# Pooled attention and a cosine-gated MLP on one core: the attention of each batch put between the second matmuls of the preceding token tile, the first matmul in pairs of columns over three two-bank PSUM tiles

## The chip, the cores and the metric

The kernel runs on one core of a Trainium2 chip. The metric is the device time of one execution in microseconds (us); the time shown for a kernel is the median of its runs.

## The reference, cut to what matters

Eight batches of 576 tokens (4608 tokens in all), 8 heads of 64. Keys and values are averaged over groups of 8 tokens, so that each head has 72 pooled keys; the attention's output, 4608 x 512, goes through an MLP without bias whose gate is h * cos(h).

```python
k_p = k.reshape(B, H, Sp, pool, D).mean(axis=3)      # Sp = 72, pool = 8
v_p = v.reshape(B, H, Sp, pool, D).mean(axis=3)
scores = scale * np.matmul(q, k_p.transpose(0, 1, 3, 2))
attn = np.exp(scores - np.max(scores, axis=-1, keepdims=True))
attn = attn / (np.sum(attn, axis=-1, keepdims=True) + 1e-09)
x = np.matmul(attn, v_p)          # then tokens x (heads * 64) = 4608 x 512
h = x @ w_in                      # w_in 512 x 2048
return (h * np.cos(h)) @ w_out    # w_out 2048 x 512
```

## The kernel before, in words

The program has two stages, one after the other, and Tile's scheduler sets the order of the instructions inside each engine's queue.

**Attention (lines 73 to 146).** For each batch, q, k and v come in chunks of 128 tokens (lines 82, 93, 99), each of them as rows of 256 bytes; ScalarE casts each chunk to bf16 (lines 84, 95, 101). TensorE transposes q (line 87), VectorE copies the transposed chunk out of PSUM with a stride of four elements on the side that it writes (line 90). TensorE pools k and v by a product with a 0/1 matrix (`pool_ext`, lines 96 and 102), and transposes the pooled keys (line 113). Then, for each pair of heads `pj` and each segment of 512 or 64 tokens, the scores of one head at a time go into `sT_ps` (line 132), ScalarE takes the exponential (line 135), two products give the sum of the exponentials, spread over 64 partitions (`cs_ps`, line 138), and the weighted values (`ao_ps`, line 140). VectorE takes the reciprocal of the sum (line 143) and multiplies (line 145); the result lies transposed in `xT_tiles`, 128 channels by 4608 tokens, four of them.

**MLP (lines 150 to 205).** The weights are loaded and cast (lines 155, 156, 162, 163). For each of nine tiles of 512 tokens, 16 chunks of 128 hidden channels are worked through: four matmuls of 512 columns into `h_ps` (line 178), the cosine as a sine with a bias (line 186), the product with h (line 189), and four matmuls into the four output blocks `out_ps` (line 193), which gather over all 16 chunks. At the tile's end ScalarE copies the four blocks out (line 204) and they are stored (line 205). There are thus 64 "first" matmuls (line 178) and 64 "second" ones (line 193) for each tile, 1152 in all.

PSUM has eight banks of 128 partitions x 512 f32. In the MLP stage three are used for `h_ps` and four for `out_ps`; the attention's PSUM pool is closed first (line 148).

Of the kernel before, what the change touches and what calls it, by code (L numbers as in the profile page):

```python
# [10 lines left out]
BF16 = mybir.dt.bfloat16  # L12


@with_exitstack
def kernel(
# [11 lines left out]
    POOL = 8  # L28
# [5 lines left out]

    assert d_model == moe_w_in.shape[0]
    assert moe_w_out.shape == (d_ff, d_model)
    assert out.shape == (n_tokens, d_model)
# [9 lines left out]
    ones_mat = consts.tile([128, 128], BF16, name="ones_mat")  # L47
    nc.gpsimd.memset(ones_mat, float(POOL))

# [3 lines left out]
    n_pool_cols = 136  # L53
    pool_ext = consts.tile([128, n_pool_cols], BF16, name="pool_ext")
    nc.gpsimd.memset(pool_ext, 1.0)
    nc.gpsimd.affine_select(pool_ext, pool_ext, pattern=[[-8, n_pool_cols]],
                            compare_op=mybir.AluOpType.is_ge, fill=0.0,
                            base=512, channel_multiplier=1)
    nc.gpsimd.affine_select(pool_ext, pool_ext, pattern=[[8, n_pool_cols]],
                            compare_op=mybir.AluOpType.is_gt, fill=0.0,  # L60
                            base=-504, channel_multiplier=-1)

    xT_pool = ctx.enter_context(tc.tile_pool(name="xT", bufs=1))
    xT_tiles = [xT_pool.tile([128, n_tokens], BF16, name=f"xT_{ki}") for ki in range(KCH)]

    s_chunk_bounds = list(range(0, S, 128)) + [S]
    NSC = len(s_chunk_bounds) - 1

    asb = ctx.enter_context(tc.tile_pool(name="asb", bufs=2))
    attn_ctx = ExitStack()  # L70
    aps = attn_ctx.enter_context(tc.tile_pool(name="aps", bufs=1, space=bass.MemoryType.PSUM))

    for b in range(B):
        qT = asb.tile([128, S, KCH], BF16, tag="qT")
        kp_ps = aps.tile([Sp, H * D], FP32, name="kp_ps", tag="kp_ps")
        vp_ps = aps.tile([Sp, H * D], FP32, name="vp_ps", tag="vp_ps")
        for ci in range(NSC):
            s0, s1 = s_chunk_bounds[ci], s_chunk_bounds[ci + 1]
            sc = s1 - s0
            pool_slice = pool_ext[:sc, 64 - 16 * ci: 64 - 16 * ci + Sp]  # L80
            qc_f = asb.tile([128, H, D], FP32, tag="qc_f")
            nc.sync.dma_start(out=qc_f[:sc, :, :], in_=q[b, :, s0:s1, :].rearrange("h s d -> s h d"))
            q_chunk = asb.tile([128, H * D], BF16, tag="q_chunk")
            nc.scalar.copy(out=q_chunk[:sc, :], in_=qc_f[:sc, :, :].rearrange("s h d -> s (h d)"))  # L84
            qT_ps = aps.tile([128, KCH, 128], BF16, name="qT_ps", tag="qT_ps")
            for pj in range(KCH):
                nc.tensor.matmul(qT_ps[:128, pj, :sc],  # L87
                                 q_chunk[:sc, pj * 128:(pj + 1) * 128], identity[:sc, :sc],
                                 is_transpose=True)
            nc.vector.tensor_copy(out=qT[:, s0:s1, :].rearrange("p s j -> p j s"),  # L90
                                  in_=qT_ps[:128, :KCH, :sc])
# [12 lines left out]

        kp = asb.tile([Sp, H * D], BF16, tag="kp")
        nc.scalar.copy(out=kp, in_=kp_ps[:Sp, :])
        vp = asb.tile([Sp, H * D], BF16, tag="vp")
        nc.scalar.copy(out=vp, in_=vp_ps[:Sp, :])

        kpT = asb.tile([128, KCH, Sp], BF16, tag="kpT")  # L110
# [125 lines left out]
```

## Time and profile before

| what | us |
|---|---|
| median of 3 runs (lowest, highest) | 547.68 (547.28, 548.22) |
| span of the profiled execution | 544.7 |
| attention and weights, to the first matmul of line 178 | 273.0 |
| MLP, from there to the span's end | 271.7 |
| busy: TensorE, VectorE, ScalarE, GpSimd | 442.7, 296.6, 247.2, 1.6 |

The span of the profiled execution runs from its first to its last instruction; its own device time is not among the three runs, and the median of these lies 3.0 us above its span. PE stands for TensorE's matmuls, PEld for its weight loads, DVE for VectorE, ACT for ScalarE, POOL for GpSimd, SPq for the queue of the engine that issues the loads and stores. In a group's row, "x" is the count, then come busy time and the mean time of one; behind the bar, the idle time of the engine just before, and what ended it. The mean time of a matmul is its latency: matmuls overlap, so that eight of them which take 0.38 us each can stand in 1.73 us.

### The profile page before, as it was taken

Reading aid. Unit: us, or ns where it says so; the run is one execution under the profiler, and the core shown is the slowest. Engines: PE = TensorE matmul, PEld = TensorE weight load, DVE = VectorE, ACT = ScalarE, POOL = GpSimd, SP = SyncE. Lnnn points to the kernel's source line nnn. Section 1 sums busy time; section 2 is a strip of 40 time slices with the busy share of each in tenths; the row PEclk is TensorE's granted clock in tenths of the full one; section 3 lists DMA queues with packets and bytes.
Section 4 is the critical chain, followed back from the end, with each engine's and each line's share of the span. In section 5 each row is a group of like instructions: output and inputs, shape, how many; then the busy total and the mean of one; then the engine's idle time right before and its main releaser. Section 6 shows DMA issues by size and latency. Waiting matters only on the chain.

```text
span 544.7 us, 5181 instructions
## 1 busy us (share of the span) xinstructions
PE 442.7 (81%) x1808; PEld 167.6 (31%) x1808; DVE 296.6 (54%) x332; ACT 247.2 (45%) x454; POOL 1.6 (0%) x11
## 2 busy tenths in 40 slices
PE   3675866758686676745599999999999999999994
PEld 1222223222222222212233333333333433343331
DVE  2387676867867686786865334433443344334431
ACT  4554454555445464522233535453444435443543
POOL 1000000000000000000000000000000000000000
PEclk9999999999999999999999999999999999999998
DMA  9955538464465755705043201010020202020202
GB/s 191 207 113 124 119 87 154 102 136 91 97 135 124 125 119 118 238 1 193 0 137 95 78 1 73 5 51 27 1 77 1 77 1 77 1 77 2 77 1 77
DMA packets 120601, 46.47 MB, mean 85 GB/s; under 512 B 113408, under 2 KB 113408, under 8 KB 120064
## 3 DMA queue, kind: packets, MB, share of 16 engines
q1 hardware_dynamic: 120576, 46.15, 35.4%
q8 instruction: 14, 0.23, 0.2%
q14 instruction: 11, 0.09, 0.0%
HBM read 36.70 MB, written 9.44 MB: 85 GB/s over the span
## 4 chain that ended last, share of the span: by engine, by line
PE 71%; ACT 9%; issue 7%; DVE 7%; DMA 4%; SPq 1%; ACTq 0%
PE out_ps L193 24%; PE h_ps L178 22%; PE sT_ps L132 9%; ACT expT L135 8%; PE cs_ps L138 6%; DVE qT L90 5%; PE ao_ps L140 3%; PE qT_ps L87 2%; PE kp_ps L96 2%; DMA kc_f<-in_k_dram 2%; PE vp_ps L102 1%; DMA wo_f<-in_moe_w_out_dram 1%; DMA vc_f<-in_v_dram 1%; DVE inv L143 1%; DVE w_in L156 1%
## 5 line engine op out<-in xcount | busy, mean ns | idle before, releaser
L189 DVE TENSOR_TENSOR g_sb<-h_ps,cos_sb 128x512 bf16<-128x512 f32 x144 | 99.5, 691 | 153.1 <-ACT cos_sb L186 153.1
L186 ACT ACTIVATE cos_sb<-h_ps,half_pi 128x512 f32<-128x512 f32 x144 | 99.1, 689 | 143.9 <-PE h_ps L178 143.9
L178 PE MATMUL h_ps<-xT,w_in 128*128 128x512 bf16 x576 | 142.8, 384 | 2.7 <-DVE xT L145 2.7
L193 PE MATMUL out_ps<-w_out,g_sb 128*128 128x512 bf16 x576 | 142.0, 380 | 2.5 <-DVE g_sb L189 2.3
L143 DVE RECIPROCAL inv<-cs_ps 128x512 f32<-128x512 f32 x64 | 120.4, 1922 | 33.9 <-PE cs_ps L138 33.9
L135 ACT ACTIVATE expT<-sT_ps 72x64 bf16<-72x64 f32 (+1 forms) x128 | 52.0, 407 | 90.3 <-PE sT_ps L132 65.9
L178 PEld LDWEIGHTS <-w_in 128*128 128x128 bf16 x576 | 56.9, 99 | 72.7 <-issue 6.2
L132 PE MATMUL sT_ps<-qT,kpT 64*72 64x64 bf16 (+1 forms) x128 | 56.1, 438 | 25.1 <-ACT expT L135 22.1
L193 PEld LDWEIGHTS <-g_sb 128*128 128x128 bf16 x576 | 46.2, 97 | 92.7 <-DVE g_sb L189 54.8
L90 DVE COPY qT<-qT_ps 128x512 bf16<-128x512 bf16 (+1 forms) x40 | 47.1, 1178 | 46.3 <-PE qT_ps L87 46.3
L138 PE MATMUL cs_ps<-expT,ones_mat 72*64 72x64 bf16 (+1 forms) x128 | 41.0, 427 | 18.5 <-ACT expT L135 17.6
L87 PE MATMUL qT_ps<-identity,q_chunk 128*128 128x128 bf16 (+1 forms) x160 | 22.9, 289 | 31.1 <-DVE qT L90 24.2
L140 PE MATMUL ao_ps<-expT,vp 72*64 72x64 bf16 (+1 forms) x128 | 40.7, 437 | 0.0
L84 ACT CAST q_chunk<-qc_f 128x512 bf16<-128x512 f32 (+1 forms) x40 | 24.5, 612 | 20.5 <-PE qT_ps L87 16.6
L87 PEld LDWEIGHTS <-q_chunk 128*128 128x128 bf16 (+1 forms) x160 | 14.1, 125 | 56.7 <-issue 39.9
L96 PE MATMUL kp_ps<-k_chunk,pool_ext 128*72 128x512 bf16 (+1 forms) x40 | 24.8, 620 | 5.5 <-ACT k_chunk L95 5.4
L102 PE MATMUL vp_ps<-v_chunk,pool_ext 128*72 128x512 bf16 (+1 forms) x40 | 24.7, 616 | 4.8 <-ACT v_chunk L101 4.5
L132 PEld LDWEIGHTS <-kpT 64*72 64x72 bf16 x128 | 14.8, 132 | 39.0 <-issue 30.0
L138 PEld LDWEIGHTS <-ones_mat 72*64 72x64 bf16 x128 | 13.9, 132 | 41.4 <-issue 39.8
L95 ACT CAST k_chunk<-kc_f 128x512 bf16<-128x512 f32 (+1 forms) x40 | 24.5, 611 | 2.5 <-DMA kc_f<-in_k_dram 2.5
L101 ACT CAST v_chunk<-vc_f 128x512 bf16<-128x512 f32 (+1 forms) x40 | 24.4, 610 | 2.5 <-DMA vc_f<-in_v_dram 2.5
L145 DVE TENSOR_TENSOR xT<-ao_ps,inv 128x512 bf16<-128x512 f32 x64 | 24.2, 419 | 0.0
(24 smaller groups left out, 79.7 us busy)
## 6 DMA issues: line engine op xcount, KB each, us to landing
out_dram<-out_sb SPq DMA_DIRECT2D x36, 256.0 KB, 2.2
qc_f<-in_q_dram SPq DMA_DIRECT2D x32, 256.0 KB, 3.2
kc_f<-in_k_dram SPq DMA_DIRECT2D x32, 256.0 KB, 3.8
vc_f<-in_v_dram SPq DMA_DIRECT2D x32, 256.0 KB, 3.8
wi_f<-in_moe_w_in_dram SPq DMA_DIRECT2D x4, 1024.0 KB, 5.5
wo_f<-in_moe_w_out_dram SPq DMA_DIRECT2D x16, 256.0 KB, 2.7
qc_f<-in_q_dram SPq DMA_DIRECT2D x8, 128.0 KB, 2.8
kc_f<-in_k_dram SPq DMA_DIRECT2D x8, 128.0 KB, 3.0
```

What stands on the lines that cost most here:

```text
L87: nc.tensor.matmul(qT_ps[:128, pj, :sc], q_chunk[:sc, pj * 128:(pj + 1) * 128], identity[:sc, :sc], is_transpose=True)
L90: nc.vector.tensor_copy(out=qT[:, s0:s1, :].rearrange("p s j -> p j s"), in_=qT_ps[:128, :KCH, :sc])
L96: nc.tensor.matmul(kp_ps[:Sp, :], lhsT=pool_slice, rhs=k_chunk[:sc, :], start=(ci == 0), stop=(ci == NSC - 1))
L132: nc.tensor.matmul(sT_ps[:Sp, :sl], lhsT=kpT[ph0:ph1, pj, :Sp], rhs=qT[ph0:ph1, seg0:seg1, pj])
L135: nc.scalar.activation(out=expT[:Sp, :sl], in_=sT_ps[:Sp, :sl], func=mybir.ActivationFunctionType.Exp, scale=scale / POOL)
L138: nc.tensor.matmul(cs_ps[ph0:ph1, :sl], lhsT=ones_mat[:Sp, :D], rhs=expT[:Sp, :sl])
L140: nc.tensor.matmul(ao_ps[ph0:ph1, :sl], lhsT=vp[:Sp, h * D:(h + 1) * D], rhs=expT[:Sp, :sl])
L143: nc.vector.reciprocal(out=inv[:, :sl], in_=cs_ps[:, :sl])
L178: nc.tensor.matmul(h_ps[:128, :m_len], lhsT=w_in_sb[ki][:, fc * 128:(fc + 1) * 128], rhs=xT_tiles[ki][:, mi:mi + m_len], start=(ki == 0), ...
L186: nc.scalar.activation(out=cos_sb[:128, :m_len], in_=h_ps[:128, :m_len], func=mybir.ActivationFunctionType.Sin, bias=half_pi[:128, :1])
L189: nc.vector.tensor_mul(out=g_sb[:128, :m_len], in0=h_ps[:128, :m_len], in1=cos_sb[:128, :m_len])
L193: nc.tensor.matmul(out_ps[ms][:m1 - m0, :d_model], lhsT=g_sb[:128, m0:m1], rhs=w_out_sb[fc][:, :d_model], start=(fc == 0), stop=(fc == FFC ...
```

## The change

The function is written anew; only the constants, the launch and the mathematics stay. What it does:

- **Order by hand.** `tc.manual_schedule()` makes each engine's queue the order in which the code is written. Waits for data and for free buffers are still put in.
- **Loads.** k and v come as one tile of 72 partitions, each with 8 heads x 8 tokens x 64 (runs of 2 KB, line 77); 512 of a batch's 576 tokens of q come as four neighbouring tokens to a partition (runs of 1 KB, line 84), the other 64 apart (line 87). Token 4n+t of a batch stands in column n of group t, and the stores at line 240 undo this by a stride in DRAM.
- **Pooling by three adds** (lines 111 to 113: 2048, 1024 and 512 elements for each of 72 partitions) instead of a matmul; the casts of q (lines 119, 121) and these adds run on GpSimd, except that batch 0 is pooled on VectorE. GpSimd also casts the four parts of `w_out` (line 264).
- **Attention in eight steps** of two heads by 288 tokens. `scores` (line 166) puts the two heads into the two banks of one PSUM tile and takes one exponential over both, 72 x 576. `values` (line 177) makes the two sums and the two weighted values in the two banks of `banks[2]`; the reciprocal becomes a logarithm and an exponential of its negative on ScalarE (lines 187, 189), and VectorE multiplies (line 191). `k_transpose`, `q_transpose` and `q_transpose_rem` come first, and copy by VectorE. In line 143 both sides of the copy are walked in the order in which they stand, so that the block of token group t and head pair j in PSUM goes to head pair t and token group j in `qT`.
- **MLP.** For a tile, `up` runs eight times: eight matmuls into a two-bank tile (three of these, `banks`, used in turn), one sine of 128 x 1024, one product of 128 x 1024 into `g_sb`, which holds the whole tile's 16 chunks and has one buffer. Then 64 second matmuls, 16 for each of four output blocks, with two single banks in turn (`obanks`), copied out by VectorE (line 231).
- **Interleaving.** Between the second matmuls of tile t, the attention of batch t+1 is issued: its three transposes before matmuls 4, 8 and 12, and then its sixteen pieces (`scores` and `values`) from matmul 16 to 53, every two or three. Batch 0 stands alone ahead of tile 0; tiles 7 and 8 have nothing between. The activation tables are switched twice a tile (lines 206, 209).

On TensorE, inside a batch of the attention stage before (around its row 312 in that engine's queue: `sT_ps` are scores, `cs_ps` sums, `ao_ps` weighted values, `kp_ps` and `vp_ps` pooled keys and values):

```order
L132 LDWEIGHTS kpT
L132 MATMUL sT_ps<-qT,kpT 72x64
L138 LDWEIGHTS ones_mat
L138 MATMUL cs_ps<-expT,ones_mat 64x512
L138 LDWEIGHTS ones_mat
L138 MATMUL cs_ps<-expT,ones_mat 64x512
L102 LDWEIGHTS pool_ext
```

and now, in tile 0, batch 1 (`obank` takes second matmuls, `bank` 94 and 95 the scores, 96 sums and weighted values):

```order
L226 MATMUL obank_98<-w_out_sb,g_sb 128x512
L171 LDWEIGHTS kpT
L171 MATMUL bank_94<-qT,kpT 72x288
L171 LDWEIGHTS kpT
L171 MATMUL bank_94<-qT,kpT 72x288
L226 LDWEIGHTS g_sb
L226 MATMUL obank_98<-w_out_sb,g_sb 128x512
```

The matmuls of the attention, which stood among others of the attention, now stand in groups of two or four between second matmuls; each group changes the shape of the weights (64x72 or 72x64 against 128x128) and changes it back.

On GpSimd, the last rows of the whole program before were

```order
L51 MEMSET half_pi 128x1
L55 MEMSET pool_ext 128x136
L56 AFFINE_SELECT pool_ext<-pool_ext 128x136
L59 AFFINE_SELECT pool_ext<-pool_ext 128x136
```

and now, from the cast of batch 0's q through batch 1:

```order
L119 CAST q_bf<-q_main 128x8x4x64
L121 CAST q_rem_bf<-q_rem 64x512
L264 CAST w_out_sb<-w_st 128x2048 x4
L111 TENSOR_TENSOR kv_st<-kv_st 72x8x256
L112 TENSOR_TENSOR kv_st<-kv_st 72x8x128
L113 TENSOR_TENSOR kp<-kv_st 72x512
L119 CAST q_bf<-q_main 128x8x4x64
L121 CAST q_rem_bf<-q_rem 64x512
L111 TENSOR_TENSOR kv_st<-kv_st 72x8x256
L112 TENSOR_TENSOR kv_st<-kv_st 72x8x128
L113 TENSOR_TENSOR vp<-kv_st 72x512
```

GpSimd, which only set up constants, now has four weight casts and then eight instructions for each batch in one queue, those of batch 1 behind the weight casts.

The diff, cut to its core (the new file's lines; what only declares is left out):

```diff
+    def pool_kv(b, which, eng, halves=1):
...
+            eng.tensor_tensor(out=s[:, :, 0:4, :], in0=s[:, :, 0:4, :], in1=s[:, :, 4:8, :], op=ADD)
+            eng.tensor_tensor(out=s[:, :, 0:2, :], in0=s[:, :, 0:2, :], in1=s[:, :, 2:4, :], op=ADD)
+            eng.tensor_tensor(out=dst[:, i * hs:(i + 1) * hs, :], in0=s[:, :, 0, :], in1=s[:, :, 1, :], op=ADD)
...
+    def q_transpose(b, bank):
...
+        ps = bank.rearrange("p a n -> p (a n)").bitcast(BF16).rearrange("p (t j n) -> p t j n", t=4, j=KCH)
+        for t in range(4):
             for pj in range(KCH):
+                nc.tensor.matmul(ps[:, t, pj, :], qb[:, t, 2 * pj:2 * pj + 2, :].rearrange("p h d -> p (h d)"),
+                                 identity, is_transpose=True)
+        c0 = col_of(b, 0)
+        nc.vector.tensor_copy(out=qT[:, :, c0:c0 + 512].rearrange("p j (t n) -> p j t n", t=4),
+                              in_=ps.rearrange("p t j n -> p j t n"))
...
+    def scores(b, i):
+        pj, sg = i // 2, i % 2
+        kpT, qT = att["kpT", b], att["qT", b]
+        pair = banks[(i + 1) % 2]
+        for hp in range(2):
+            nc.tensor.matmul(pair[:Sp, hp, :SEG], lhsT=kpT[hp * 64:hp * 64 + 64, pj, :],
+                             rhs=qT[hp * 64:hp * 64 + 64, pj, sg * SEG:(sg + 1) * SEG])
+        ex = asb.tile([Sp, 2, SEG], BF16, name="ex", tag="ex")
+        nc.scalar.activation(out=ex, in_=pair[:Sp, :, :SEG], func=ACTF.Exp, scale=scale / POOL)
...
+    def values(b, i):
...
+        cs, ao = banks[2][:, 0, :SEG], banks[2][:, 1, :SEG]
+        for hp in range(2):
+            nc.tensor.matmul(cs[hp * 64:hp * 64 + 64, :], lhsT=ones[:Sp, :], rhs=ex[:, hp, :])
+        for hp in range(2):
+            nc.tensor.matmul(ao[hp * 64:hp * 64 + 64, :], lhsT=vp[:, 2 * pj + hp, :], rhs=ex[:, hp, :])
+        lnc = asb.tile([128, SEG], FP32, name="lnc", tag="lnc")
+        nc.scalar.activation(out=lnc, in_=cs, func=ACTF.Ln)
+        inv = asb.tile([128, SEG], FP32, name="inv", tag="inv")
+        nc.scalar.activation(out=inv, in_=lnc, func=ACTF.Exp, scale=-1.0)
+        c0 = b * S + sg * SEG
+        nc.vector.tensor_mul(out=xT[:, pj, c0:c0 + SEG], in0=ao, in1=inv)
...
+    def up(t, fp):
+        h = banks[fp % 3]
+        for j in range(2):
+            fc = 2 * fp + j
             for ki in range(KCH):
+                nc.tensor.matmul(h[:, j, :], lhsT=w_in_sb[:, ki, fc * 128:(fc + 1) * 128],
+                                 rhs=xT[:, ki, t * TILE:(t + 1) * TILE],
+                                 start=(ki == 0), stop=(ki == KCH - 1))
+        cos = msb.tile([128, 2, TILE], FP32, name="cos", tag="cos")
+        nc.scalar.activation(out=cos, in_=h, func=ACTF.Sin, bias=half_pi[:, :1])
+        nc.vector.tensor_mul(out=g_sb[:, 2 * fp:2 * fp + 2, :], in0=h, in1=cos)
...
+    for cg in range(4):
+        st = w_stage[cg]
+        nc.vector.tensor_copy(out=w_in_sb[:, :, cg * 512:(cg + 1) * 512], in_=st)
+        if cg + 2 < 4:
+            w_stage.append(load_w_in(cg + 2))
+    for cg in range(4):
+        st = load_w_out(cg)
+        nc.gpsimd.tensor_copy(out=w_out_sb[:, cg * 4:(cg + 1) * 4, :], in_=st)
+    load_kv(1, "k", k)
+    load_q(1)
+    load_kv(1, "v", v)
+    pool_kv(1, "k", nc.gpsimd)
+    cast_q(1, nc.gpsimd)
+    pool_kv(1, "v", nc.gpsimd)
+    for t in range(NT):
+        b = t + 1
+        for fp in range(FFCH // 2):
+            up(t, fp)
...
+            fill = [(4 + 4 * i, f) for i, f in enumerate(early)]
+            fill += [(16 + (i * 5) // 2, f) for i, f in enumerate(main)]
...
+        for n, (ms, fc) in enumerate(mms):
+            while fi < len(fill) and fill[fi][0] <= n:
+                fill[fi][1]()
+                fi += 1
+            down_mm(ms, fc)
+            if fc == FFCH - 1:
+                down_out(t, ms)
```

The two weight staging buffers (`wst`) are shared by `w_in` and `w_out`, four parts of 1 MB each: a part's load waits until the part two places earlier has been cast. VectorE's casts of `w_in` stand behind batch 0's last product (line 191) in its queue.

More of the change, by code (lines that the diff above doesn't have):

```diff
@@ L12 @@
 BF16 = mybir.dt.bfloat16
+ACTF = mybir.ActivationFunctionType
+ADD = mybir.AluOpType.add
+POOL = 8
+TILE = 512
 @with_exitstack
@@ L27 @@
     B, H, S, D = q.shape
-    POOL = 8
     Sp = S // POOL
@@ L45 @@
     make_identity(nc, identity)
-    ones_mat = consts.tile([128, 128], BF16, name="ones_mat")
-    nc.gpsimd.memset(ones_mat, float(POOL))
+    ones = consts.tile([128, D], BF16, name="ones")
+    nc.gpsimd.memset(ones, float(POOL))
     half_pi = consts.tile([128, 1], FP32, name="half_pi")
     nc.gpsimd.memset(half_pi, math.pi / 2.0)
[L53 to L69, printed above, removed]
```

268 lines of the change are left out of this document (149 added, 119 removed).

## The prediction

> **What bounds the kernel now.** I read the page first, then the table by stage, the groups of instructions by shape, and the timeline at four places. Page and table by stage (span, then PE, PEld, DVE, ACT and POOL busy, clock, DMA share, GB/s):
>
> ```profile
> span 544.7 us, 5181 instructions
> PE 442.7 (81%) x1808; PEld 167.6 (31%) x1808; DVE 296.6 (54%) x332; ACT 247.2 (45%) x454; POOL 1.6 (0%) x11
> PEclk9999999999999999999999999999999999999998
> 3.00:239.00 236.00, 163.88 (x594) 58.37 (x595) 163.26 (x146) 121.03 (x255) 0.00 (x0) 1.00 0.64 131
> 273.00:539.00 266.00, 263.55 (x1152) 102.91 (x1151) 105.51 (x159) 116.16 (x179) 0.00 (x0) 1.00 0.12 44
> ```
>
> Two stages, each about half of the span. In the first no engine is full: PE and DVE are busy 69% of the time, ACT 51%, and they wait for each other. In the second PE is full, 1152 matmuls in 266 us, 0.231 us each. What a matmul costs in each stage stands in the groups by shape, in the chain that ended last, and in the timeline where the second stage begins:
>
> ```profile
> L178 PE MATMUL h_ps<-xT,w_in 128*128 128x512 bf16 x576 | 142.8, 384 | 2.7 <-DVE xT L145 2.7
> L138 PE MATMUL cs_ps<-expT,ones_mat 72*64 72x512 bf16 x64 | 26.3, 625 | 3.5 <-ACT expT L135 2.6
> L87 PE MATMUL qT_ps<-identity,q_chunk 128*128 128x128 bf16 x128 | 19.9, 304 | 22.8 <-DVE qT L90 16.1 <-ACT q_chunk L84 6.5
> 476.41 1.90 PE out_ps L193 x8
> 478.31 1.73 PE h_ps L178 x8
> 272.97 4.98 PE L178 MATMUL h_ps<-xT,w_in 128*128 128x512 bf16 x12 [2.65 <-DVE xT L145]
> 257.25 0.64 PE L138 MATMUL cs_ps<-expT,ones_mat 72*64 72x512 bf16 x2
> 257.68 0.64 PE L140 MATMUL ao_ps<-expT,vp 72*64 72x512 bf16 x2
> ```
>
> A run of eight first matmuls takes 1.73 us, 0.216 each; a run of eight second ones 1.90. In the attention the same 512 columns take 625 ns where the MLP shows 384, and the first twelve of the MLP take 4.98 us, 0.41 each: PE runs at about half speed there, and for the first dozen dense matmuls after it, though the granted clock reads 1.00 throughout. And two sums for the two halves of PSUM's partitions lie on top of each other: two pairs, four matmuls, from 257.25 to 258.32, the second pair 0.43 after the first.
>
> So the floor of the change is PE at full speed: 1152 x 0.216 = 249 us, plus the attention's matmuls.
>
> **The first matmuls.** `up` has 64 in a row: 64 x 0.216 = 13.8 us. Beside them run eight sines and eight products of 1024:
>
> ```profile
> L186 ACT ACTIVATE cos_sb<-h_ps,half_pi 128x512 f32<-128x512 f32 x144 | 99.1, 689 | 143.9 <-PE h_ps L178 143.9
> L189 DVE TENSOR_TENSOR g_sb<-h_ps,cos_sb 128x512 bf16<-128x512 f32 x144 | 99.5, 691 | 153.1 <-ACT cos_sb L186 153.1
> L135 ACT ACTIVATE expT<-sT_ps 72x512 bf16<-72x512 f32 x64 | 38.0, 593 | 43.8 <-PE sT_ps L132 43.8
> L135 ACT ACTIVATE expT<-sT_ps 72x64 bf16<-72x64 f32 x64 | 14.1, 220 | 46.5 <-PE ao_ps L140 22.9 <-PE sT_ps L132 22.1
> L145 DVE TENSOR_TENSOR xT<-ao_ps,inv 128x512 bf16<-128x512 f32 x32 | 20.1, 627 | 0.0
> L145 DVE TENSOR_TENSOR xT<-ao_ps,inv 128x64 bf16<-128x64 f32 x32 | 6.7, 210 | 0.0
> 536.18 0.38 PE L178 MATMUL h_ps<-xT,w_in 128*128 128x512 bf16 x1
> 536.60 0.69 ACT L186 ACTIVATE cos_sb<-h_ps,half_pi 128x512 f32<-128x512 f32 x1 [2.07 <-PE h_ps L178]
> 537.32 0.69 DVE L189 TENSOR_TENSOR g_sb<-h_ps,cos_sb 128x512 bf16<-128x512 f32 x1 [2.07 <-ACT cos_sb L186]
> 538.06 1.04 PE L193 MATMUL out_ps<-w_out,g_sb 128*128 128x512 bf16 x4 [1.50 <-DVE g_sb L189]
> ```
>
> By the two shapes ACT takes 0.83 ns a column over a start of 0.17 us, DVE 0.93 over 0.15. The sine of 1024 then costs 0.69 + 0.43 = 1.12, the product 0.69 + 0.48 = 1.17. A two-bank tile comes free 0.2 + 1.12 + 1.17 + 0.1 = 2.6 us after its matmuls end; PE wants it 2 x 1.73 = 3.45 us after. Hidden, 0.9 to spare; without that, PE would pay the difference eight times a tile. The last product ends 2.6 us after `up`, and matmul 14 wants it 3.0 after: hidden too.
>
> **The second matmuls with the attention.** 64 x 0.216 = 13.8 again. A pair of 288 columns costs 288/512 x 0.216 = 0.121 if its halves overlap, as the sums do above (for the halves of the rows, in `scores`, no row shows it: at most 0.243, and I take 0.121). Eight steps of one such pair and of two in `values`: 8 x 0.363 = 2.9.
>
> Each of the sixteen pieces changes the shape of the weights and back. At the slow speed the timeline shows one such change, from scores to sums:
>
> ```profile
> 250.45 0.64 PE L132 MATMUL sT_ps<-qT,kpT 64*72 64x512 bf16 x1
> 251.02 0.13 PEld L138 LDWEIGHTS <-ones_mat 72*64 72x64 bf16 x1 [0.44 <-issue]
> L193 PEld LDWEIGHTS <-g_sb 128*128 128x128 bf16 x576 | 46.2, 97 | 92.7 <-DVE g_sb L189 54.8 <-issue 1.6
> ```
>
> The load begins 0.57 after a matmul of 0.43 of columns, and takes 0.13: up to 0.27 for a change. At full speed the nearest row is the run of 1.90 against 1.73: weight loads of `g_sb` there wait on a semaphore, are not pulled ahead, and such a run costs 0.17 more, though nothing changes its shape. Between nothing and 0.27 I take 0.16, the full speed's row: 32 x 0.16 = 5.1 us a tile. [...]
>
> A step is five second matmuls, three pairs and four changes: 1.08 + 0.36 + 0.64 = 2.08 us. Beside it goes a ring through one PSUM tile, `banks[2]`: sums, logarithm 0.17 + 288 x 0.83 ns = 0.41, exponential 0.41, product 0.15 + 0.27 = 0.42, next sums. With 0.4 from PE's start to ACT (536.18 to 536.60 above) and 0.14 for three handovers, 1.78 us: hidden, by 0.3. ACT itself needs 0.65 + 0.41 + 0.41 = 1.47 a step. The reciprocals that go are DVE's busiest group, and their place is taken by 0.82 of ACT a step, under PE.
>
> Ahead of the steps stand 16 second matmuls (3.45), 24 transposes (2.0: q's sixteen took 19.9/128 = 0.155 each at the slow speed, 0.10 is my estimate for the full one, and 0.05 for the eight smaller) and two changes: 5.8 of PE. But the copy of `qT` is later: q's last transpose ends 8 x 0.216 + 0.2 + 1.6 + 0.4 = 3.9 us into the stretch.
>
> ```profile
> L90 DVE COPY qT<-qT_ps 128x512 bf16<-128x512 bf16 x32 | 41.3, 1291 | 41.7 <-PE qT_ps L87 41.7
> L143 DVE RECIPROCAL inv<-cs_ps 128x512 f32<-128x512 f32 x64 | 120.4, 1922 | 33.9 <-PE cs_ps L138 33.9
> L186 ACT ACT_TABLE_LOAD x1 | 1.3, 1283 | 5.0 <-PE h_ps L178 5.0
> ```
>
> The copy of 2048 per partition costs 2048 x 0.93 + 0.15 = 2.06 if written in runs, up to 4.7 at the strided row's (1291 - 150)/512 = 2.2 ns. I take 2.06, since runs are what the product's row has. With the copy of the rest (0.39) the first scores start at 6.5. The table loads, 1.28 twice a tile, lie where ACT has 5 us free (sines end at 1.4, the first exponential is at 6.8) and under the last 11 second matmuls (2.4 us); exposed, 14 would cost 18.
>
> The rest: 48 x 0.216 + 2.9 + 5.1 = 18.4. **A tile with attention:** 13.8 + 6.5 + 18.4 = 38.7 us. Without: 27.6. The copies of the output blocks move from ACT to DVE (0.63 each by the product's row, four a tile), which has about 18 us of work in 38.7. The stores stand on SP behind the loads of the next batch, which wait for buffers that POOL has read a tile earlier; the store's landing is waited for only three blocks later.
>
> **The start.** Loads, casts, POOL:
>
> ```profile
> GB/s 191 207 113 124 119 87 154 102 136 91 97 135 124 125 119 118 238 1 193 0 137 95 78 1 73 5 51 27 1 77 1 77 1 77 1 77 2 77 1 77
> 3.87 0.62 ACT L84 CAST q_chunk<-qc_f 128x512 bf16<-128x512 f32 x1 [1.79 <-DMA qc_f<-in_q_dram]
> wi_f<-in_moe_w_in_dram SPq DMA_DIRECT2D x4, 1024.0 KB, 5.5
> L156 DVE CAST w_in<-wi_f 128x2048 bf16<-128x2048 f32 x4 | 5.0, 1238 | 1.8 <-DMA wi_f<-in_moe_w_in_dram 1.8
> L56 POOL TENSOR_SCALAR_AFFINE_SELECT pool_ext<-pool_ext 128x136 bf16<-128x136 bf16 x1 | 0.3, 299 | 0.1
> L51 POOL MEMSET half_pi<- 128x1 f32 x1 | 0.1, 100 | 0.0
> ```
>
> The first 256 KB are there at 3.87 us; at 238 GB/s, the most of any slice, k of batch 0 (1.18 MB) has landed at about 7.7 us, q's main part at 12.2, v at 17.6. POOL has no add and no cast in the trace. Its nearest row, a select with one input, gives (299 - 100)/135 = 1.46 ns an element; for the casts I take that, for adds with two inputs between it and twice it, 2.2 (1.46 to 2.9). So: cast of q 3.7, adds of 3584 elements 7.9 us, a weight cast 3.1. [...]
>
> Casts on POOL to 15.9; transposes at the slow rate and copies to 19.7; pooling of v on DVE, 2 x 2.1, to 23.9; eight steps of the ring, which no second matmul covers and where PE is slow, 1.93 each (the ring with 0.15 more), to 39.3; first weight cast, 40.5. Then the staging: parts 2 and 3 of `w_in` are requested only now, and DVE has their casts ahead of the first product, until 48.5. PE, which has filled three tiles, goes on at 49.7 and ends `up` at 58.4. `w_out` goes through the same two buffers and POOL: casts end at 55.9, 59.0, 64.5, 67.6. Batch 1's loads queue behind the last of these on SP; k lands at 69.4. POOL then works 7.9 + 3.7 + 7.9 = 19.5 to 88.9, while PE stands at batch 1's transposes and then its first `values`. What is left of tile 0 is 46 second matmuls and 14 pieces, 17.0, and 2.2 for PE's slow beginning: 108.1. In later tiles POOL's 19.5 lie under 38.7.
>
> **Sum.** Tiles 1 to 6 6 x 38.7 = 232.2; tiles 7 and 8 2 x 27.65 = 55.3. The end:
>
> ```profile
> 541.23 0.59 ACT L204 COPY out_sb<-out_ps 128x512 f32<-128x512 f32 x1 [1.18 <-DMA out_dram<-out_sb]
> ```
>
> 2.85 us lie between this copy's end and the span's; with the last matmul and the copy 3.9. 108.1 + 232.2 + 55.3 + 3.9 = 399.5 of span, against 544.7. The median of the runs shown, 547.68, lies 3.0 above the profiled span: 402.5, which I round to **402 us**.
>
> **The rivals.**
> - *The changes of shape cost almost nothing* (0.03), because weight loads are pulled ahead across them. For it: on equal shapes a load is hidden wholly. 220 changes x 0.13 = 28 less: 374. Chance 0.13.
> - *The ring sets the step.* It decides from 2.08 us; at 2.6, should each of ACT's two dependent steps wait 0.4 for the one before, 56 x 0.52 = 29 more: 431. The handovers of 0.03 to 0.05 in the timeline speak against it. 0.12.
> - *PE falls back to its slow speed* in the mixed stretches: 16.7 us of streaming a tile doubled, 7 x 16.7 = 117 more: 519. Against it: after 1.50 us of idling at 538.06, four matmuls still took 1.04 us. 0.05.
> - *POOL becomes the bound, and the kernel slower.* If a batch takes P on POOL, batch 7's values come no sooner than 69.4 + 7P, and the end is at 69.4 + 7P + 17.0 + 55.3 + 3.9 + 3.0 = 148.6 + 7P. It binds from P = 36 and passes 548.8 from P = 57.2, 2.9 times my 19.5. In place of the eleven tiny instructions that the trace shows, POOL gets strided adds in place; nothing excludes it. 0.05 for 36 to 57 (402 to 548), 0.03 beyond.
>
> The forecast has the remaining 0.62. That the interleaving isn't made is no rival: the instructions stand so in PE's queue.
>
> **Range and chances.** Unknown costs inside the forecast: changes at 0.27 +24, scores not overlapping +7, the `qT` copy +16, POOL's adds ±5, loads ±5. From 368 (first rival and a quicker start) to 436 (the ring); beyond it lie the clock, most of POOL, and tails. Faster by over 0.2% (1.1 us, about what runs of this kernel can tell apart) in all but POOL's last case, 0.97; within it in none, since no case ends near 548; slower 0.03.
>
> **What would show it.** Right: a period of 38 to 39 us from tile to tile; pieces without waits for ACT or DVE; about 0.16 lost by PE at each change; one long wait of PE for POOL between 60 and 89 us. Wrong: PE waiting for the product of line 191 in every step (ring), 512 columns at 586 or more in the mixed stretches (clock), waits for POOL in each tile (POOL), or changes without gaps.

## The result, and the profile after

| | before | after |
|---|---|---|
| median (lowest, highest; 4 runs each) | 547.48 (547.16, 548.22) | 387.62 (387.41, 389.72) |
| ratio of the two, with its 95% interval | | 0.7091 (0.7073 to 0.7108) |
| profiled execution: time, span | | 387.81, 385.9 |

The forecast was 402 with a range of 368 to 436: the sign and the range held, the size came out 14 us too high. One sentence of the part on the change has to be corrected: line 143 reads its source as `"p t j n -> p j t n"`, so the block of token group t and head pair j goes where it belongs, to head pair j and token group t. No term of the sum hangs on it.

The page of the changed kernel (span, TensorE, the clock granted in 40 slices):

```profile
span 385.9 us, 4455 instructions
PE 326.0 (84%) x1728; PEld 134.5 (35%) x1728; DVE 167.9 (44%) x212; ACT 191.9 (50%) x280; POOL 141.3 (37%) x70
PEclk9999969568999999999999999999999999999999
```

TensorE was busy for 442.7 us before and is for 326.0 now. The 80 matmuls of the pooling are gone, and from batch 2 on the attention's others, which ran at about half speed (a pair of sums of 512 columns 0.43 us, 0.84 ns a column), run at full speed between the second matmuls (a pair of 288 columns 0.14 us, 0.49 ns a column, in the rows of tile 2 below). The granted clock is low only in slice 6 (0.6) and slices 8 to 10 (0.5, 0.6, 0.8), about 48 to 58 and 68 to 96 us: that is tile 0, where TensorE stands for 4.1, 14.7 and 2.3 us. The row does not show every slow stretch: in batch 0 it reads 9, while sixteen transposes take 1.83 us (15.16 to 16.99) and 0.89 in tile 2 below.

The chain that ended last (start, duration, engine, tile, line, count; the long pieces):

```profile
107.14 13.81 PE bank L218 x64
...
143.71 13.81 PE bank L218 x64
...
326.56 13.81 PE bank L218 x64
...
354.19 13.81 PE bank L218 x64
368.00 13.83 PE obank L226 x64
```

Tile 0 ends at 107.14; a tile with attention takes 36.57 (143.71 less 107.14, six times to 326.56); tiles 7 and 8 take 27.64 each, and 4.1 us follow to the span's end.

The transposes of q, one step, and the last values of the interleaved stretch in tile 2 (start, duration, engine, line, operation, tiles, count; in brackets idle time of that engine before it):

```profile
159.22 1.06 PE L140 MATMUL bank<-identity,q_bf 128*128 128x128 bf16 x16
...
160.11 1.03 PE L226 MATMUL obank<-w_out_sb,g_sb 128*128 128x512 bf16 x4
...
162.26 0.31 PE L171 MATMUL bank<-qT,kpT 64*72 64x288 bf16 x2
162.50 0.61 PE L226 MATMUL obank<-w_out_sb,g_sb 128*128 128x512 bf16 x2
163.04 0.31 PE L171 MATMUL bank<-qT,kpT 64*72 64x288 bf16 x2
163.29 0.82 PE L226 MATMUL obank<-w_out_sb,g_sb 128*128 128x512 bf16 x3
164.04 0.31 PE L183 MATMUL bank<-ex,ones 72*64 72x288 bf16 x2
164.18 0.29 PE L185 MATMUL bank<-ex,vp 72*64 72x288 bf16 x2
164.41 0.60 PE L226 MATMUL obank<-w_out_sb,g_sb 128*128 128x512 bf16 x2
164.51 0.41 ACT L187 ACTIVATE lnc<-bank 128x288 f32<-128x288 f32 x1 [0.47 <-PE bank L185]
164.96 0.44 ACT L189 ACTIVATE inv<-lnc 128x288 f32<-128x288 f32 x1
165.43 0.46 DVE L191 TENSOR_TENSOR xT<-bank,inv 128x288 bf16<-128x288 f32 x1 [2.38 <-ACT inv L189]
165.94 0.31 PE L183 MATMUL bank<-ex,ones 72*64 72x288 bf16 x2
...
177.36 0.31 PE L183 MATMUL bank<-ex,ones 72*64 72x288 bf16 x2 [0.93 <-DVE xT L191]
```

A step takes 1.90 us (164.04 to 165.94). The ring of sums, logarithm, exponential and product takes the same 1.90: it starts with the sums at 164.04, the product ends at 165.89, and the next sums follow 0.05 later. TensorE's own work fills that time too: in the rows between no wait is shown. Only before the last values of a tile, with no scores between the two last pieces, does it wait 0.93 us.

The groups of that stretch and of GpSimd, whose instructions before were eleven tiny ones (the last two numbers are busy time and mean ns of one, then idle time before):

```profile
L111 POOL TENSOR_TENSOR kv_st<-kv_st 72x2048 f32<-72x2048 f32 x14 | 63.2, 4518 | 87.4 <-DMA kv_st<-in_k_dram 82.7
L119 POOL CAST q_bf<-q_main 128x2048 bf16<-128x2048 f32 x8 | 15.1, 1889 | 11.8 <-DMA q_main<-in_q_dram 11.8
L143 DVE COPY qT<-bank 128x2048 bf16<-128x2048 bf16 x8 | 9.8, 1225 | 8.9 <-PE bank L140 8.9
```

And TensorE's waits at the start (us in all, times, longest):

```profile
PE bank L161 <- POOL kp L113: 14.7, 1, 14.7
PE bank L140 <- POOL q_bf L119: 3.2, 1, 3.2
PE bank L185 <- POOL vp L113: 2.3, 1, 2.3
```

TensorE waits for GpSimd once for batch 0's q (3.2 us) and otherwise in tile 0 alone. Later GpSimd waits itself, for k (82.7 us in all).

### The profile page after: what moved, and what is told of

Read it like the earlier page. It is cut to its first block, busy times and chain, and to the rows that moved or that the text cites. A ratio compares the mean times of both kernels' runs of the same rounds, so it can differ in the third digit from the quotient of the medians.

```text
span 385.9 us, 4455 instructions
## 1 busy us (share of the span) xinstructions
PE 326.0 (84%) x1728; PEld 134.5 (35%) x1728; DVE 167.9 (44%) x212; ACT 191.9 (50%) x280; POOL 141.3 (37%) x70
## 4 chain that ended last, share of the span: by engine, by line
PE 75%; DMA 12%; DVE 4%; ACT 3%; POOL 3%; SPq 1%; issue 1%; POOLq 0%
PE obank L226 34%; PE bank L218 29%; DMA kv_st<-in_v_dram 5%; PE bank L183 4%; PE bank L171 3%; DMA q_main<-in_q_dram 3%; PE bank L185 2%; DMA w_st<-in_moe_w_in_dram 2%; PE bank L140 2%; DVE xT L191 2%; ACT inv L189 2%; ACT lnc L187 2%; DMA w_st<-in_moe_w_out_dram 1%; POOL kv_st L111 1%; DVE w_in_sb L259 1%
## 5 line engine op out<-in xcount | busy, mean ns | idle before, releaser
L226 PE MATMUL obank<-w_out_sb,g_sb 128*128 128x512 bf16 x576 | 151.5, 387 | 0.0
L218 PE MATMUL bank<-xT,w_in_sb 128*128 128x512 bf16 x576 | 130.6, 389 | 6.7 <-DVE g_sb L223 4.1
L222 ACT ACTIVATE cos<-bank,half_pi 128x1024 f32<-128x1024 f32 x72 | 80.3, 1115 | 78.4 <-PE bank L218 78.4
L223 DVE TENSOR_TENSOR g_sb<-bank,cos 128x1024 bf16<-128x1024 f32 x72 | 88.0, 1224 | 51.4 <-ACT cos L222 51.4
L111 POOL TENSOR_TENSOR kv_st<-kv_st 72x2048 f32<-72x2048 f32 x14 | 63.2, 4518 | 87.4 <-DMA kv_st<-in_k_dram 82.7
L218 PEld LDWEIGHTS <-w_in_sb 128*128 128x128 bf16 x576 | 57.4, 100 | 78.6 <-issue 10.6
L191 DVE TENSOR_TENSOR xT<-bank,inv 128x288 bf16<-128x288 f32 x64 | 29.3, 458 | 94.9 <-ACT inv L189 94.9
L174 ACT ACTIVATE ex<-bank 72x576 bf16<-72x576 f32 x64 | 40.8, 640 | 54.4 <-PE bank L171 53.4
L183 PE MATMUL bank<-ex,ones 72*64 72x288 bf16 x128 | 21.3, 324 | 15.7 <-DVE xT L191 15.2
L112 POOL TENSOR_TENSOR kv_st<-kv_st 72x1024 f32<-72x1024 f32 x14 | 32.9, 2349 | 1.1
L189 ACT ACTIVATE inv<-lnc 128x288 f32<-128x288 f32 x64 | 28.3, 442 | 2.0
L161 PE MATMUL bank<-identity,kp 72*128 72x72 bf16 x32 | 2.8, 208 | 26.0 <-POOL kp L113 14.7
```

What stands on the lines that cost most here:

```text
L111: eng.tensor_tensor(out=s[:, :, 0:4, :], in0=s[:, :, 0:4, :], in1=s[:, :, 4:8, :], op=ADD)
L112: eng.tensor_tensor(out=s[:, :, 0:2, :], in0=s[:, :, 0:2, :], in1=s[:, :, 2:4, :], op=ADD)
L174: nc.scalar.activation(out=ex, in_=pair[:Sp, :, :SEG], func=ACTF.Exp, scale=scale / POOL)
L183: nc.tensor.matmul(cs[hp * 64:hp * 64 + 64, :], lhsT=ones[:Sp, :], rhs=ex[:, hp, :])
L189: nc.scalar.activation(out=inv, in_=lnc, func=ACTF.Exp, scale=-1.0)
L191: nc.vector.tensor_mul(out=xT[:, pj, c0:c0 + SEG], in0=ao, in1=inv)
```

## The experiments

Each run was timed beside the kernel before; ratios are to that kernel, with their 95% interval. The theory behind the forecast: TensorE at full speed sets the time once the attention lies between second matmuls; the ring is just hidden; tile 0 waits for loads, casts and GpSimd. Rivals: the interleaving is not what counts, the ring or GpSimd binds.

**The attention apart.** The same pieces, all of them behind the 64 second matmuls.

```diff
-            fill = [(4 + 4 * i, f) for i, f in enumerate(early)]
-            fill += [(16 + (i * 5) // 2, f) for i, f in enumerate(main)]
+            fill = [(64, f) for f in early]
+            fill += [(64, f) for f in main]
```

> The attention of batch t+1 is issued behind all 64 second matmuls of tile t, instead of between them; everything else stays. Theory: the interleaving hides the ring of sums, logarithm, exponential, product (1.90 us a step in the changed kernel's trace) under second matmuls. Without that cover a batch costs its transposes and copies (about 3.5) and 8 ring steps (15.2) on top of 27.6, against the 8.9 that it adds now: 10 us more for each of tiles 1 to 6, up to 13 where TensorE slows down and has to warm up again; tile 0 loses little, since its second matmuls then run while TensorE would wait for GpSimd. 448 to 466 us. Rival, that the gain lies in the other parts (loads in long runs, pooling and transposes off TensorE, no long reciprocal) and the order matters little: 385 to 395 us.

Measured 476.44, ratio 0.8712 (0.8695 to 0.8730). The table by stage, for one tile: `up`, second matmuls, attention (after the bounds: length, busy time and count of PE, PEld, DVE, ACT and POOL, the granted clock, DMA share, GB/s):

```profile
219.00:234.00 15.00, 14.95 (x60) 6.34 (x61) 7.68 (x7) 8.47 (x8) 0.00 (x0) 0.87 0.02 5
234.00:248.00 14.00, 13.95 (x69) 6.41 (x69) 4.19 (x5) 2.40 (x2) 0.00 (x0) 1.00 0.19 57
248.00:267.00 19.00, 8.99 (x73) 4.60 (x71) 5.53 (x11) 10.63 (x23) 17.57 (x8) 0.65 0.81 179
```

This order costs 89 us of the 160 that the change gains, more than either side expected. In tiles 1 to 6 two things cost, together 11.7 us a tile: TensorE is busy for 9 of the 19 us of attention, since the ring has nothing beside it, and the granted clock falls to 0.65 there, so that the next `up` is slower as well. The `up` of the first row begins 1.2 us ahead of the window and takes 16.27 us in all (217.78 to 234.05), where the changed kernel's takes 13.81. Tile 0 loses 15.3 us, against the expectation, and there the waits show a third thing (us in all, times, longest):

```profile
DVE o_sb L231 <- DMA out_dram<-o_sb: 26.2, 1, 26.2
```

VectorE's copy of an output block waits for the store of an earlier one, which stands in SP's queue behind the loads of batch 2, and the copies of the transposes stand behind it. So not all of the 89 us is cover: part of tile 0's share comes from the order of that queue. The clock, which the third rival feared inside the mixed stretches, is lost when the attention stands alone: 0.65 in the third row, 1.00 in the changed kernel's tile 2 (157.5 to 180.2 us).

**The reciprocal on VectorE again.**

```diff
-        nc.scalar.activation(out=lnc, in_=cs, func=ACTF.Ln)
-        nc.scalar.activation(out=inv, in_=lnc, func=ACTF.Exp, scale=-1.0)
+        nc.vector.reciprocal(out=inv, in_=cs)
```

> The logarithm and the exponential of its negative are replaced by VectorE's reciprocal, as before the change. By the rows of before (3350 ns for 512, 494 for 64) it takes 1.93 us for 288. Theory: the ring through the one sums-and-values tile then takes 2.95 us instead of 1.90, second matmuls cover only 1.90 of it, and TensorE waits about 1.05 in each of 64 steps: 67 us more, about 455 us. If TensorE alone sets the step and the ring does not bind: 388 us.

Measured 460.85, ratio 0.8427 (0.8395 to 0.8460). Two rounds of the ring in its timeline:

```profile
191.62 1.96 DVE L187 RECIPROCAL inv<-bank 128x288 f32<-128x288 f32 x1 [1.46 <-PE bank L185]
193.61 0.46 DVE L189 TENSOR_TENSOR xT<-bank,inv 128x288 bf16<-128x288 f32 x1
194.12 0.31 PE L183 MATMUL bank<-ex,ones 72*64 72x288 bf16 x2 [1.01 <-DVE xT L189]
194.60 1.96 DVE L187 RECIPROCAL inv<-bank 128x288 f32<-128x288 f32 x1 [0.53 <-PE bank L185]
```

The ring is 2.98 (191.62 to 194.60), and TensorE waits 1.01 in every step. Swapping one instruction of 1.96 for two of 0.41 and 0.44 is worth 73 us of the change.

**The pieces closer together**, three second matmuls to a step instead of five.

```diff
-            fill += [(16 + (i * 5) // 2, f) for i, f in enumerate(main)]
+            fill += [(16 + (i * 3) // 2, f) for i, f in enumerate(main)]
```

> Three second matmuls for each step instead of five, so that the last pieces stand at matmul 38 and not 53; the work is the same. Theory of a ring at 1.90 us: TensorE needs only 1.47 for a step, so that it waits 0.43 in each, and 1.2 instead of 0.93 before the last; 3.4 us a tile, 24 in all: 411 us. Theory that TensorE alone sets the step: the wait before the last piece stays and nothing else changes, 387 to 389 us.

Measured 420.05, ratio 0.7681 (0.7664 to 0.7699). Its timeline, and the table by stage for the second matmuls that are left over at the end of the stretch:

```profile
139.41 0.31 PE L183 MATMUL bank<-ex,ones 72*64 72x288 bf16 x2 [0.36 <-DVE xT L191]
...
141.32 0.31 PE L183 MATMUL bank<-ex,ones 72*64 72x288 bf16 x2 [0.37 <-DVE xT L191]
```

```profile
145.50:153.20 7.70, 7.68 (x29) 3.18 (x29) 1.35 (x3) 2.14 (x3) 0.00 (x0) 0.78 0.10 36
```

The step stays at 1.90, though TensorE has 0.43 less to do: the ring sets it, as the theory said. The cost is higher than expected, 32 us: 5.0 in tile 0, 4.5 in each of the next six tiles (41.06 instead of 36.57). Part of that is in the row of the table: after a stretch with a wait in every step the granted clock is 0.78 for 7.7 us. Of the matmuls there, about eight start 0.43 us apart instead of 0.216, which is 1.7 us a tile.

**The last values four matmuls later.**

```diff
-            fill += [(16 + (i * 5) // 2, f) for i, f in enumerate(main)]
+            fill += [(16 + (i * 5) // 2 + (4 if i == 15 else 0), f) for i, f in enumerate(main)]
```

> Only the last piece, values of step 7, is moved from second matmul 53 to 57. In the changed kernel's trace TensorE waits 0.93 us there in each tile for the product of step 6, since no scores stand between the last two pieces. Theory: four more matmuls cover all but 0.15 of it, and the seven left behind it still cover the way to the next tile's first matmul: 0.75 x 7 = 5 us less, 382.4 us. Rival: the wait only moves to the first matmul of the next tile, which needs the last product: 387 to 388 us.

Measured 383.05, ratio 0.7003 (0.6988 to 0.7018). Its chain:

```profile
143.37 13.81 PE bank L218 x64
179.08 13.81 PE bank L218 x64
```

The tile takes 35.71 instead of 36.57: the wait of 0.93 is gone, and nothing else came late.

**Scores and values side by side**, to halve the number of groups; the last values stay at matmul 57.

```diff
-            fill += [(16 + (i * 5) // 2, f) for i, f in enumerate(main)]
+            fill += [(16 if i == 0 else 57 if i == 15 else 19 + ((i - 1) // 2) * 11 // 2, f) for i, f in enumerate(main)]
```

> As the run with the late last piece, and the scores of step i+1 stand directly ahead of the values of step i, every 5.5 second matmuls, so that a step has three changes of the weights' shape instead of four. Theory: a change costs 0.107 us (half of what the trace shows for going there and back); 7 x 0.107 a tile, 5 us less than the run with the late last piece: about 377 us. If a change between the two attention shapes costs as much as two, or weight loads are the cause and not the change: no difference to that run, 382 us.

Measured 386.23, ratio 0.7059 (0.7043 to 0.7076): 3 us above the run before. Its timeline:

```profile
162.21 0.31 PE L171 MATMUL bank<-qT,kpT 64*72 64x288 bf16 x2
162.45 0.31 PE L183 MATMUL bank<-ex,ones 72*64 72x288 bf16 x2
...
164.53 0.31 PE L183 MATMUL bank<-ex,ones 72*64 72x288 bf16 x2 [0.21 <-DVE xT L191]
...
176.78 0.31 PE L183 MATMUL bank<-ex,ones 72*64 72x288 bf16 x2 [0.45 <-DVE xT L191]
```

Both sides missed. From scores to sums 0.24 us pass, for 0.121 of columns: this change of shape (64 x 72 to 72 x 64) costs 0.12, as much as one to the full square, so a step does save one change of four, as the theory had it. But the pieces now come every five or six matmuls in turn: in the shorter gap the ring is 0.21 late, three times in this tile, and it is 0.45 late before the last values. These 1.08 us are more than the saved changes bring, and a tile takes 36.17 us (142.66 to 178.83 in the chain) instead of 35.71.

**Columns of 512 in the same pair tiles.**

```diff
-        cos = msb.tile([128, 2, TILE], FP32, name="cos", tag="cos")
-        nc.scalar.activation(out=cos, in_=h, func=ACTF.Sin, bias=half_pi[:, :1])
-        nc.vector.tensor_mul(out=g_sb[:, 2 * fp:2 * fp + 2, :], in0=h, in1=cos)
+            cos = msb.tile([128, TILE], FP32, name="cos", tag="cos")
+            nc.scalar.activation(out=cos, in_=h[:, j, :], func=ACTF.Sin, bias=half_pi[:, :1])
+            nc.vector.tensor_mul(out=g_sb[:, fc, :], in0=h[:, j, :], in1=cos)
```

> The sine and the product are done per 512 columns again, 16 of each in a tile, on the same three two-bank tiles. Theory: with 16 x 0.69 us, ScalarE and VectorE need 11.0 of the 13.8 us of first matmuls, so that they stay hidden and nothing changes: 386.5 to 388.5 us. Rival, that the pairs carry part of the gain (two more instruction starts and handovers for each pair, 0.35 us, eight times a tile): 25 us more, 412 us.

Measured 500.48, ratio 0.9137 (0.9100 to 0.9175), far from both. Its timeline, and its waits:

```profile
179.10 0.69 DVE L223 TENSOR_TENSOR g_sb<-bank,cos 128x512 bf16<-128x512 f32 x1 [1.83 <-ACT cos L222]
180.02 0.69 DVE L223 TENSOR_TENSOR g_sb<-bank,cos 128x512 bf16<-128x512 f32 x1 [0.23 <-ACT cos L222]
180.77 1.89 PE L218 MATMUL bank<-xT,w_in_sb 128*128 128x512 bf16 x7 [1.56 <-DVE g_sb L223]
```

```profile
PE bank L218 <- DVE g_sb L223: 117.7, 72, 7.7
```

TensorE waits 72 times, once in each pair: the second four matmuls write the other bank, but the tile is one, and in this kernel the wait goes by the tile, so they wait for the product of the first half. These waits, 117.7 us in all, account for the 113 that the run loses. That left open whether pairs are good for anything else.

**Columns of 512, each in a tile of its own**, three in turn.

```diff
-        h = banks[fp % 3]
         for j in range(2):
             fc = 2 * fp + j
+            h = banks[fc % 3][:, 0, :]
```

(with the sine and the product as in the run before)

> The sine and the product go by 512 columns again, and each goes into a PSUM tile of its own, three in turn, one bank of each (the other three banks are idle in the first matmuls). Theory: the run with single columns in pair tiles lost its 113 us only because the second four matmuls waited for the product of the first half of the same tile. Here a tile comes free 0.2 + 0.69 + 0.69 + 0.1 = 1.68 us after its matmuls (sine and product of 512 by the rows of the kernel before), and TensorE wants it two columns later, 2 x 0.864 = 1.73: nothing or a few hundredths of a us each for 144 columns, 387 to 391 us. The rival: the doubled instructions themselves cost, by their start of 0.15 to 0.17 us each for 72 more sines and 72 more products on the way from matmul to matmul: 72 x 0.3 = 22, about 410 us.

Measured 388.83, ratio 0.7103 (0.7088 to 0.7118), which overlaps the changed kernel's 0.7091 (0.7073 to 0.7108). The pairs alone bring nothing that can be told; they halve the number of sines and products and, by the estimates, leave more room before TensorE wants a bank back (0.9 us against 0.05).

**The casts of `w_in` on GpSimd.** They stood on VectorE behind batch 0's last product.

```diff
-        nc.vector.tensor_copy(out=w_in_sb[:, :, cg * 512:(cg + 1) * 512], in_=st)
+        nc.gpsimd.tensor_copy(out=w_in_sb[:, :, cg * 512:(cg + 1) * 512], in_=st)
```

> The four casts of w_in go from VectorE, where they stand behind batch 0's last product, to GpSimd, which is idle from 15.7 to 52 us. Theory: the start is a chain through two staging buffers; the first two parts then leave them at about 24 and 28 us instead of 39 and 41, each later load comes earlier, batch 1's keys are pooled from about 56 us instead of 70, and values of batch 1 can start at 75 instead of 90: 15 us less, 372 to 374 us. Rival: transfers at the start are bound by bandwidth (about 240 GB/s), and the chain moves by only a few us: 383 us or more.

Measured 373.63, ratio 0.6827 (0.6804 to 0.6850). Its chain:

```profile
46.62 20.58 DMA kv_st<-in_v_dram
...
94.58 13.81 PE bank L218 x64
```

Tile 0 ends at 94.58 instead of 107.14: the staging buffers come free during the attention, so all later loads start sooner. What is left ahead of tile 0's end is batch 1's v.

**GpSimd at about 50 us a batch**: from batch 2 on, the cast of q is written sixteen more times with the same data.

```diff
+                for _ in range(16):
+                    nc.gpsimd.tensor_copy(out=pooled["q", b + 1][0].rearrange("p t h d -> p h t d"), in_=qm)
```

> For batches 2 to 7 GpSimd repeats the cast of q 16 times more, with the same result, so that its work for a batch rises from 19 to about 48 us; nothing else changes. This tries the rival that GpSimd becomes the bound. By its formula, with the changed kernel's own rows: values of batch 1 may start at 89.5, those of batch 7 at 89.5 + 6 x 48.2 = 378.7, then 17.7 for the rest of that tile, 55.3 for the last two tiles, 4.1 for the end and 1.7 outside the span: 457 us. If GpSimd's work were hidden whatever it is, 388 us.

Measured 468.04, ratio 0.8561 (0.8542 to 0.8579). Its chain:

```profile
131.91 4.47 POOL kv_st L111
...
181.95 4.47 POOL kv_st L111
```

A batch takes 50.04 on GpSimd, 2 more than the 48 that the expectation went by, and six times 2 are the 11 us by which it was short. The rival of the forecast is a real mechanism; the kernel is not near it, with some 18.8 us a batch (two poolings of 4.52 + 2.35 + 1.26, casts of 1.89 + 0.61).

**Both edits that helped, together** (`w_in` on GpSimd, last values at matmul 57).

> The two single edits that helped, together: w_in cast on GpSimd, and the last values at second matmul 57. They act in different places (ahead of tile 0, and at the end of each second stretch), so the theory adds them: 387.6 - 14.0 - 4.6 = 369.0 us, 368 to 370. The rival: the wait before the last values is only cover for something that is late next, batch 1's v on GpSimd in tile 0 at least, so that less than the sum comes: 372 to 374.

Measured 367.80, ratio 0.6729 (0.6709 to 0.6749), 1.2 us below the sum: they add.

**Batch 1 on VectorE as well**, its loads ahead of batch 2's.

```diff
-    pool_kv(1, "k", nc.gpsimd)
     cast_q(1, nc.gpsimd)
-    pool_kv(1, "v", nc.gpsimd)
...
+            if t == 0:
+                pool_kv(1, "k", nc.vector, 2)
+                fill.insert(3, (12, lambda: pool_kv(1, "v", nc.vector, 2)))
+            else:
+                next_loads()
...
+                if t == 0 and ms == 0:
+                    next_loads()
```

> As the run with both edits, and batch 1 comes sooner: its k and v are loaded in halves and pooled on VectorE (k behind tile 0's products, v behind the copies of qT), GpSimd only casts its q, and the loads of batch 2 are issued behind the first stored block of tile 0 instead of ahead of it. In the run with w_in on GpSimd, batch 1's k landed at 55.5 and its pooling ended at 63.8, v landed at 67.2 and was pooled at 75.6; tile 0 ended at 94.6. Theory (tile 0 ends a fixed 19 us behind batch 1's pooled v): v lands at about 61, since batch 2's k no longer shares the DMA engines, the second half is pooled in 2.3 us, and TensorE goes on at 64 to 65 instead of 75.7: 369 - 11 = 358 us, 356 to 361. The rival: the loads set it, since v lands at 67 still (as much is loaded before it): TensorE goes on at 69.6, 369 - 6 = 363 us or more.

Measured 362.30, ratio 0.6621 (0.6610 to 0.6632): between the two. Rows of its timeline at that place, first of VectorE, then of GpSimd:

```profile
56.48 0.69 DVE L112 TENSOR_TENSOR kv_st<-kv_st 72x512 f32<-72x512 f32 x1
...
58.79 2.40 DVE L112 TENSOR_TENSOR kv_st<-kv_st 72x512 f32<-72x512 f32 x1
...
58.76 1.89 POOL L119 CAST q_bf<-q_main 128x2048 bf16<-128x2048 f32 x1 [8.63 <-DMA q_main<-in_q_dram]
60.60 1.07 POOL L121 CAST q_rem_bf<-q_rem 64x512 bf16<-64x512 f32 x1
```

The same add takes 0.69 and 2.40; the slow one starts 0.03 behind a cast on GpSimd and ends 0.54 after it. Batch 1's k was late by that, and its v by VectorE's queue.

**The same, with batch 1's q cast by ScalarE and half of v pooled ahead of the copies of `qT`.**

```diff
-    cast_q(1, nc.gpsimd)
...
-                fill.insert(3, (12, lambda: pool_kv(1, "v", nc.vector, 2)))
+                fill.insert(1, (4, lambda: pool_kv(1, "v", nc.vector, 2, 0)))
+                fill.insert(4, (12, lambda: pool_kv(1, "v", nc.vector, 2, 1)))
...
+            if t == 0:
+                cast_q(1, nc.scalar)
```

> As the run with batch 1 pooled on VectorE, with two edits in tile 0 alone: ScalarE casts batch 1's q instead of GpSimd, and VectorE pools the first half of v before the copies of qT instead of behind them. In the run before, VectorE's add of 512 elements (line 112) took 2.40 us instead of 0.69 while GpSimd cast q (58.76 to 60.65), and v's second half was pooled at 72.6 though the last load landed at about 64.4. Theory: VectorE and GpSimd hold each other up when both read SBUF, so that without the cast the add takes 0.69 again, kp is there at 60 instead of 62, v at 68.4 instead of 72.6, and tile 0 ends 3 to 4 us sooner: 358 to 360 us (362.3 before). The rival: the add was slow for another reason (loads landing in SBUF at the same time, which are unchanged): its 2.40 us stays, and only v's order brings something, 360 to 362 us.

Measured 359.44 (358.90 to 360.72, 5 runs), ratio 0.6579 (0.6567 to 0.6591). The same add in its timeline, and then its chain:

```profile
59.69 0.69 DVE L112 TENSOR_TENSOR kv_st<-kv_st 72x512 f32<-72x512 f32 x1
```

```profile
84.59 13.81 PE bank L219 x64
```

0.69 again, with the loads issued as before. The DMA engines were as busy beside a fast add: in the run before, the add of k's first half took 0.69 at 56.48 with these engines busy for 0.8 of the time, against 0.7 to 0.8 beside the slow one. It was the cast. Tile 0 ends at 84.59. This is the fastest version, 34.2% below the kernel before where the change is 29.1% below. From there to the end TensorE shows no wait in the profile; what is left is the start.

## Why the prediction was right, and where its size was off

The sum came to 402.5 and the kernel took 387.6. The difference of 14.9, by its terms:

- **A tile with attention**, 38.7 in the sum, 36.57 measured: six times 2.13, 12.8 of the 14.9. This is the mis-sized term, and it has two parts.
  - *First scores 6.5 into the stretch*: 4.74 (162.26 less the end of `up`, 143.71 + 13.81). The copy of `qT` took 1.225 where I took 2.06 by the product's row. That row reads f32, the copy bf16; a copy of f32 from PSUM, line 231, takes 0.69 for 512, so that the type is the likely reason. And the sixteen transposes run through in 0.89 (159.22 to 160.11), 0.056 each, where I estimated 0.10. These two are 1.5 of the 1.8 us.
  - *The rest 18.4*: 18.02. A step is 1.90 and not 2.08, because a change of shape costs about 0.11: five second matmuls are 1.08, the three pairs 0.36, and 0.46 is left for four changes. Singly they can be read off the step above: 162.26 to 162.50 less 0.121 is 0.12, 163.29 to 164.04 less 3 x 0.216 is 0.10. Between sums and values (164.04 to 164.18), where the weights change and their shape does not, it is 0.02: the change of shape costs, not the new weights. I took 0.16, the run of waiting weight loads, between nothing and 0.27; no row of before shows a change at full speed. For 32 changes at 0.115 that is 1.4 us less, of which the 0.93 ahead of the last values takes most again. I had not looked for that wait: I checked the ring against a whole step, and the last two pieces have only half of one between them. The run with later last values takes this wait away, and 0.86 us a tile with it.
- **Tile 0 ends at 108.1**: 107.14. That this agrees to 1 us is in part luck. GpSimd's casts of q took 2.5 and of a weight part 1.9 instead of 3.7 and 3.1, and the last cast of `w_out` ended at 65.0 instead of 67.6; but k of batch 1 then took longer to land, and its pooling began at 69.97 (forecast 69.4). From there GpSimd's 19.5 us to the pooled v came as forecast, a pooling at 8.1 instead of 7.9. What counts at the start is when a staging buffer comes free, as the run with `w_in` on GpSimd shows.
- **Tiles 7 and 8, the tail**: 55.27 and 4.1 against 55.3 and 3.9. **Outside the span** 1.9 in the profiled execution, 1.7 by the median, instead of 3.0.

Of the signs that the forecast named, two came: the pieces run without waits for ScalarE or VectorE, but for the 0.93 before the last, and TensorE's long wait for GpSimd is there (14.7 us, to 78.27). Two missed: the period is 36.57 and not 38 to 39, and a change costs 0.11 and not 0.16. Two slips in the working change nothing: (299 - 100)/135 is 1.47, and 1.90 less 1.73 is 0.17.

The rivals: *changes cost almost nothing* is out by the same numbers, though the time lay halfway to it. *The ring sets the step* did not come true at 2.6, but the two stand level at 1.90; at three matmuls to a step, or with the reciprocal, it does set it. I had it 0.3 below the step; handovers and the start of the logarithm (0.47 behind the sums) made it 1.90 instead of 1.78. *PE falls back to its slow speed*: not in the mixed stretches (granted clock 1.00 in tile 2), but where they are thinned by waits (0.78 for 7.7 us in the dense run) or missing (0.65 in the run with the attention apart). *POOL* has half of the tile to spare.

What the change consists of: the new form with the attention apart gains 71 us and the interleaving 89 more, of which 15 fall in tile 0; with the reciprocal of before, 73 of the whole would be lost. The pairs that the change is also named by bring nothing measurable.

## What to carry to other kernels

Where a chain through several engines leaves TensorE idle half of the time, as the attention apart did (busy for 9 of 19 us), independent matmuls put between its links can pay twice, as they did here: they filled the gaps and kept the clock up (granted 1.00 instead of 0.65). Space them so that TensorE's work between two links is no shorter than the chain's own round (with 0.43 less than the ring's 1.90 it waited 0.36 in nearly every step), and check the irregular places, first and last links above all. Before one engine is given work to relieve another, look at which buffers its queue holds back, and at what the other reads at that moment (an add of 0.69 us took 2.40 beside a cast).

## What the runs showed of the hardware that was not expected

- **VectorE and GpSimd slowed each other.** An add with both inputs in SBUF took 2.40 us instead of 0.69 beside a cast on GpSimd, and 0.69 again without. GpSimd's small cast took 1.07 instead of 0.61 there. VectorE's product of line 223, which reads one side from PSUM, stays at 1.22 to 1.23 also while GpSimd adds. What makes the two slow, no run here shows.
- **The clock fell with short waits too.** Waits of 0.36 in each step of 1.90, and one of 1.14, were followed by eight matmuls at half rate (0.43 us apart instead of 0.216, 3.4 us in all), in a tile of the dense run; the single 0.93 of the changed kernel was not (granted clock 1.00 in the 15.7 us behind it). How much idling it takes, no run here tells exactly.
- **VectorE's reciprocal** takes 6.8 ns a column (1.96 us for 288) where its product takes 1.6 (0.46).
